# A fused attention, SoLU layer and softplus layer on one core: the planned order computed anew with other transfer costs, LayerNorm weights loaded as rows, and wide early fillers

## The chip, the cores and the metric

The kernel runs on one core of one Trainium2 chip, as one program. The metric is device time in microseconds (us), the median of three runs. One further execution was profiled; all durations below come from it.

## The reference

Three stages follow each other on 4 batches of 576 tokens, 512 wide:

```
scores = q k^T / 8, masked           # 8 heads of 64: heads 0-3 see the last 32 tokens,
attn   = softmax(scores) v           # heads 4-7 every 4th of the last 128
h   = x w_in                         # layer 1: 512 -> 1024
s   = h * softmax(h)
ln  = (s - mean(s)) / sqrt(var(s) + 1e-6) * g_ln
x   = ln w_out                       # 1024 -> 512
out = softplus(x w2_in) w2_out       # layer 2: 512 -> 2048 -> 512
```

The weights arrive as 64-bit floats, q, k and v as 32-bit floats. The output is 2304 x 512, float32.

## The kernel before, in words

**Arithmetic.** The large products run in fp16 with each operand split into a high and a low half, three products for one (high x high, high x low, low x high). A weight piece of 128 x 512 comes in as 512 KB of 64-bit words (`weights`, a DMA of 128 x 1024 words); DVE turns it into 32-bit floats in three steps (`to_f32`: a short TENSOR_SCALAR at L634, two long SCALAR_TENSOR_TENSOR at L637), ACT sums its squares, and when all pieces of a matrix are summed, PE adds over partitions and DVE makes a power-of-two scale (the chain that begins with the TENSOR_REDUCE at L811). Then the high half (ACT or DVE) and the low half (DVE) are written into the resident tile `W`. Parts of `W` and `E` that are not yet in use serve as buffers for raw pieces and for the float32 pieces, so a transfer `W<-in_moe_w_in_dram` is a raw piece on its way in. Layer 1 has eight pieces for `w_in` and eight for `w_out` (names `w1i`, `w1o`), layer 2 four quarters of four and four (`w2i0` to `w2i3`, `w2o0` to `w2o3`).

**Attention.** 28 pairs of blocks (`pair`). The first ten (`pair32`) run in float32: PE turns q and k (L652, four to a block of heads), ACT or DVE copies them from PSUM, PE makes the scores, DVE takes maxima (L1085), ACT the exponentials. The other 18 (`block`) work on fp16 halves, which the DMA turns (`dma_t`, `DMA_TRANSPOSE`). Their results go into the ring `xr`.

**Layers.** 18 tiles of 128 tokens go through layer 1's first product (`m1`: two halves, `ps_w<-W,xr`), the softmax and LayerNorm on DVE (the row maximum at L1320 is its first step) and ACT, and a DMA transpose. Groups of two tiles go through the second product (`y_stage`) and layer 2 (`mlp2`: eight hidden parts and eight output parts).

**The order.** Nothing is issued as written. The functions record operations with costs in a `Plan`; `Plan.order` goes through them with a clock of its own, hands each engine the ready operation with the earliest due time (`TABLE`, one number for each operation, in tenths of us), and the program is then written in that order, with `keep_in_program_order`, so each engine runs its own list in order. All transfers go through SP's list. Costs: `dma_cost(issue, land)`, `moving(packets, size, lag)` for a transfer's share of the DMA engines, `pe_cost` and others for compute. When PE has nothing to do in that plan before 400 us, the plan puts in a filler, emitted at L1572 as eight matmuls of 60 columns that nothing reads:

```
        if o is None:
            for _ in range(8):
                pin(nc.tensor.matmul(banks[1][:, 452:512], eye, eye[:, 0:60], start=False, stop=False, skip_group_check=True))
            continue
```

There are 190 of these groups. `g_ln` (1024 numbers) is loaded with one transfer whose elements are single numbers, into `gT` of 128 x 8; it is the scale in the squares of `w1o` and enters `sg`, the scale of its halves.

Of the kernel before, what the change touches and what calls it, by code (L numbers as in the profile page):

```python
# [65 lines left out]
class Plan:  # L66
# [12 lines left out]
    SWITCH = 1.4  # L79
    CLING = 20.0  # L80
# [64 lines left out]
    def order(self):  # L145
# [13 lines left out]
        idle_at = dict.fromkeys(self.ENGINES, 0.0)  # L159
        over, out, events = set(), [], [0.0]  # L160
        ends = []
        moved = 0.0
        tab = 1
# [7 lines left out]
        while events:  # L171
# [17 lines left out]
            while again:  # L189
                again = False  # L190
                for e in self.ENGINES:
# [56 lines left out]
                    if o.mv:  # L248
                        moved = max(moved, now + c) + o.mv
                        o.t1 = max(o.t1, moved + o.lag)  # L250
# [34 lines left out]
def moving(packets, size, lag=2.4):  # L285

    return packets * (12 + size / 21.0) / 16000, lag
# [3 lines left out]
def kernel(  # L291
# [1316 lines left out]
```

## Time and profile before

| | |
|---|---|
| median of 3 runs | 731.29 us (729.33 to 731.72) |
| the profiled execution | 730.25 us, span of its instructions 728.5 us |
| PE busy | 702.1 us, 96% of the span, fillers included |
| DVE busy | 510.5 us, 70% |
| ACT busy | 457.1 us, 63% |
| DMA | 90.0 MB moved, mean 124 GB/s |

The page cuts the span into 40 equal slices of 18.2 us and gives the busy share of each engine in tenths. DVE's digits are 3 and 5 in the first two slices, 8 and 9 with few exceptions up to the fourteenth, and then fall to between 1 and 9; PE's are 6 in the first slice and 8 or 9 in nearly all others. The DMA engines are at 8 in the first two slices. Busy time of PE counts a matmul from its start to its modelled end, so consecutive matmuls overlap. A row of a timeline gives start, length, engine, line of the kernel, operation and tiles, the count of merged instructions, and in brackets the idle time of the engine before it with what ended that. "PEclk" is the granted clock of PE as a share of 2.4 GHz.

### The profile page before, as it was taken

How to read it: one execution, taken by the hardware profiler on the slowest of the kernel's cores; microseconds unless marked ns; L12 is line 12 of the kernel's file. 1: busy time of each engine (PE TensorE's matmuls, PEld its weight loads, DVE VectorE, ACT ScalarE, POOL GpSimd, SP SyncE). 2: the span in 40 equal slices, each digit the busy share in tenths (PEclk: the TensorE clock that was granted, in tenths of full speed). 3: DMA queues.
4: the chain of work that ended last, by engine and by line, in shares of the span. 5: the costliest groups of instructions: out<-in, count | busy, mean ns of one | idle time of the engine just before them, and what ended most of it. 6: DMA issues, size and time to landing. Idle time of an engine off the chain costs nothing.

```text
span 728.5 us, 17028 instructions
## 1 busy us (share of the span) xinstructions
PE 702.1 (96%) x6697; PEld 508.8 (70%) x6697; DVE 510.5 (70%) x1558; ACT 457.1 (63%) x913; POOL 3.5 (0%) x22
## 2 busy tenths in 40 slices
PE   6988999999999899999999999999999999999997
PEld 6875577877676468777765776776668767657764
DVE  3598999999999883957988973289994372651221
ACT  1677798689899666758886673378972444521112
POOL 1000000000000000000000000000000000000000
PEclk9967999999999999999999999999999999999999
DMA  8869776587995535666776481068641111110001
GB/s 228 239 186 252 229 171 158 151 174 159 186 197 118 149 114 160 163 171 130 169 143 140 102 172 51 10 135 170 133 95 40 34 31 33 31 37 23 1 1 58
DMA packets 187808, 89.98 MB, mean 124 GB/s; under 512 B 158032, under 2 KB 175440, under 8 KB 187728
## 3 DMA queue, kind: packets, MB, share of 16 engines
q1 hardware_dynamic: 187728, 88.90, 52.5%
q8 instruction: 52, 0.85, 0.5%
q14 instruction: 28, 0.23, 0.1%
HBM read 54.53 MB, written 4.72 MB: 81 GB/s over the span
## 4 chain that ended last, share of the span: by engine, by line
PE 68%; DVE 17%; ACT 5%; DMA 5%; issue 3%; POOL 0%; SPq 0%; ACTq 0%; POOLq 0%; DVEq 0%
PE bank L646 35%; PE ps_w L646 28%; DVE W L637 5%; PE bank L1572 4%; DVE E L637 2%; DMA E<-in_moe_w_in_dram 1%; PE bank L652 1%; DMA W<-in_moe_w_out_dram 1%; ACT s L628 1%; DMA pT<-p 1%; DVE s L1194 1%; DVE g L637 1%; ACT L1576 1%; DVE p L640 1%; DVE hl L640 1%
## 5 line engine op out<-in xcount | busy, mean ns | idle before, releaser
L646 PEld LDWEIGHTS <-W 128*128 128x128 f16 x2592 | 252.0, 98 | 35.6
L646 PE MATMUL bank<-y,W 128*128 128x256 f16 x1728 | 197.6, 273 | 0.0
L646 PE MATMUL ps_w<-W,g 128*128 128x512 f16 x864 | 195.4, 379 | 0.0
L646 PEld LDWEIGHTS <-g 128*128 128x128 f16 x864 | 83.2, 98 | 90.3
L646 PE MATMUL ps_w<-W,xr 128*128 128x512 f16 x432 | 100.2, 386 | 2.5 <-DMA xr<-x 2.5
L628 ACT ACTIVATE r<-bank,invC 128x512 f32<-128x512 f32 x72 | 49.2, 685 | 83.5 <-PE bank L646 81.0
L646 PE MATMUL bank<-lnT,W 128*128 128x256 f16 x864 | 96.6, 273 | 0.0
L637 DVE SCALAR_TENSOR_TENSOR g<-r,KR,g 128x512 f16<-128x512 f32 x72 | 53.6, 747 | 40.9 <-ACT g L628 39.1
L1576 ACT ACT_TABLE_LOAD x61 | 78.3, 1283 | 1.1
L646 PEld LDWEIGHTS <-xr 128*128 128x128 f16 x432 | 42.3, 100 | 51.0 <-issue 3.7
L1572 PE MATMUL bank<-eye 128*128 128x60 bf16 x1520 | 55.4, 196 | 8.4 <-issue 2.1
L1572 PEld LDWEIGHTS <-eye 128*128 128x128 bf16 x1520 | 52.5, 102 | 10.3 <-issue 9.9
L628 ACT ACTIVATE s<-s 96x128 f32<-96x128 f32 (+3 forms) x144 | 43.6, 375 | 15.2 <-DVE s L634 11.3
L628 ACT ACTIVATE E<-E 128x768 f32<-128x768 f32 (+3 forms) x52 | 38.3, 737 | 18.1 <-issue 5.5
L632 DVE TENSOR_SCALAR g<-r,KR 128x512 f16<-128x512 f32 x36 | 17.3, 481 | 45.9 <-PE ps_w L646 40.6
L1194 DVE CUSTOM_DVE_ANT_0 s<-bank,band,bsc 96x128 f32<-96x128 f32 (+3 forms) x144 | 39.0, 325 | 7.9 <-PE bank L646 7.7
L628 ACT ACTIVATE y<-bank 128x512 f16<-128x512 f32 x17 | 10.1, 593 | 41.5 <-PE bank L646 41.5
L628 ACT ACTIVATE e<-ps_w,st,bsc 128x1024 f32<-128x1024 f32 x16 | 19.2, 1203 | 24.4 <-DVE st L632 13.5
L637 DVE SCALAR_TENSOR_TENSOR y<-bank,y 128x512 f16<-128x512 f32 x18 | 12.3, 684 | 29.9 <-ACT y L628 29.9
L628 ACT ACTIVATE g<-r,KR 128x512 f16<-128x512 f32 x36 | 25.7, 719 | 9.1 <-PE ps_w L646 8.3
L1320 DVE TENSOR_REDUCE st<-ps_w 128x1 f32<-128x1024 f32 x18 | 21.9, 1219 | 10.0 <-PE ps_w L646 10.0
L637 DVE SCALAR_TENSOR_TENSOR E<-E 128x512 int32<-128x512 int32 x42 | 27.8, 686 | 0.0
(191 smaller groups left out, 864.7 us busy)
## 6 DMA issues: line engine op xcount, KB each, us to landing
E<-in_moe_w_in_dram SPq DMA_DIRECT2D x18, 512.0 KB, 4.7
E<-in_moe_w_out_dram SPq DMA_DIRECT2D x18, 512.0 KB, 4.4
out_dram<-osb SPq DMA_DIRECT2D x18, 256.0 KB, 2.4
E<-in_v_dram SPq DMA_DIRECT2D x9, 384.0 KB, 3.3
E<-in_q_dram SPq DMA_DIRECT2D x9, 384.0 KB, 3.2
E<-in_k_dram SPq DMA_DIRECT2D x9, 384.0 KB, 4.0
W<-in_moe_w_in_dram SPq DMA_DIRECT2D x6, 512.0 KB, 7.5
W<-in_moe_w_out_dram SPq DMA_DIRECT2D x6, 512.0 KB, 4.7
```

The costliest lines, as they stand in the source:

```text
L628: pin(nc.scalar.activation(out=out, in_=in_, func=func, **kw))
L632: pin(nc.vector.tensor_scalar(out=out, in0=in0, scalar1=s1, scalar2=None, op0=op0))
L637: pin(nc.vector.scalar_tensor_tensor(out=out, in0=in0, scalar=s, in1=in1, op0=op0, op1=op1, **kw))
L640: pin(nc.vector.tensor_tensor(out=out, in0=a, in1=b, op=op))
L646: pin(nc.tensor.matmul(out, l, r, start=start, stop=stop))
L652: pin(nc.tensor.transpose(out, in_, eye32[:in_.shape[0], :in_.shape[0]]))
L1194: pin(nc.vector.tensor_tensor_reduce(out=sv()[:rows, h, :nk], in0=sb.t[:rows, h, :nk], in1=band[:rows, 48 - m:48 - m + nk], scale=sc[:rows ...
L1320: ({"DVE": (1.142, 0.14)}, lambda e: pin(nc.vector.tensor_reduce(out=col(0), in_=ph(), axis=AXX, op=ALU.max, negate=True)), [mb], [ps]),
L1572: pin(nc.tensor.matmul(banks[1][:, 452:512], eye, eye[:, 0:60], start=False, stop=False, skip_group_check=True))
L1576: pin(nc.scalar.preload_act_table_set(TABLES[tab]))
```

## The change

Four things change in the code. First, the planner's picture of transfers: engines start at times of their own (`START`), at most eight transfers may be under way (`LANES`, a pool that every SP operation takes a slot of), moving data takes 7% longer per packet, ordinary transfers have a `lag` of 2.2 in place of 2.4 and begin to occupy the DMA engines half a microsecond after their issue begins (`LEAD`), and the transposes get issue times, landing times and lags of their own. Second, with these costs the due times of all operations (`TABLE`, 2522 numbers) are new, so all five lists have a new order. Third, `g_ln` comes as eight rows of 128 numbers into a buffer of the `e` pool, is turned by PE and copied into `gT` by ACT or DVE. Fourth, fillers that stand ahead of the first use of a `ps_w` buffer are one matmul of 512 columns into that buffer.

```diff
@@ class Plan
+    LATE, LEAD = 2.0, 0.5
+    LANES = 8
+    START = {"PE": 4.3, "ACT": 2.0, "DVE": 1.0, "SP": 0.8}
@@ Plan.order
-        idle_at = dict.fromkeys(self.ENGINES, 0.0)
-        over, out, events = set(), [], [0.0]
+        idle_at = dict(self.START)
+        over, out, events = set(), [], sorted(self.START.values())
...
-                        moved = max(moved, now + c) + o.mv
+                        moved = max(moved, now + (c if o.lag > self.LATE else self.LEAD)) + o.mv
@@ moving
-def moving(packets, size, lag=2.4):
-    return packets * (12 + size / 21.0) / 16000, lag
+def moving(packets, size, lag=2.2):
+    return 1.07 * packets * (12 + size / 21.0) / 16000, lag
@@ the table of due times: all of its numbers
-        487, 164, 133, 150, 174, 167, 195, 207, 226, 218, 189, 136, 212, 239, 216, 308, 261, 332, 331, 305, 382,
...
@@ g_ln
-    g_load = P.op("gT", dma_cost(0.5, 4.0), lambda e: dma(gT, g_ln.rearrange("(c p) -> p c", p=128)), due=("w1o", -20))
+    gb, gp = Buf(e_pool), Buf(ps_x)
+    g_load = P.op(
+        "gl", dma_cost(0.4, 2.0), lambda e: dma(gb.t[:K1, 0:128], g_ln.rearrange("(c p) -> c p", p=128)), uses=[gb], mv=moving(8, 512),
+    )
+    g_turn = P.op("gt", pe_cost(0.1), lambda e: turned(gp.t[:, 0:K1], gb.t[:K1, 0:128]), after=[g_load], uses=[gb, gp])
+    g_load = P.op("gT", {**act_cost(K1, psum=1), **dve_cost(K1, x=1)}, lambda e: cast(e, gT, gp.t[:, 0:K1]), after=[g_turn], uses=[gp], due=("w1o", -20))
@@ costs of transfers, one of each kind
-                f"{name}.{i}l", dma_cost(0.4, 3.0),
+                f"{name}.{i}l", dma_cost(0.4, 3.5),
...
-                    f"ld{n}.{x}", dma_cost(0.5, 3.0), load, uses=[buf], mv=moving(4 * cnt, 512),
+                    f"ld{n}.{x}", dma_cost(0.4, 2.4), load, uses=[buf], mv=moving(4 * cnt, 512),
...
-            after=[q_h, q_l, q_d, q_c], uses=[qk, qt], mv=moving(16 * rows, 256, 0.7),
+            after=[q_h, q_l, q_d, q_c], uses=[qk, qt], mv=moving(16 * rows, 256, 1.6),
...
-            after=[ll], uses=[hl, ln], mv=moving(16 * 128, 256, 0.0),
+            after=[ll], uses=[hl, ln], mv=moving(16 * 128, 256, 1.2),
@@ end of the kernel function
+    lanes = Pool("lanes", [None] * P.LANES, fifo=False)
+    for o in P.ops:
+        if "SP" in o.opts:
+            buf = Buf(lanes)
+            o.uses.append(buf)
+            buf.left += 1
+            buf.users.append(o)
     order = P.order()
-    tab = 1
+    tab, unused = 1, True
     mm(banks[1][:, 452:512], eye, eye[:, 0:60], True, True)
     for o in order:
         if o is None:
+            if unused:
+                mm(ps_w.slots[0][0][:, 0], eye, eye.unsqueeze(1).broadcast_to([128, 4, 128]), True, True)
+                continue
             for _ in range(8):
                 pin(nc.tensor.matmul(banks[1][:, 452:512], eye, eye[:, 0:60], start=False, stop=False, skip_group_check=True))
             continue
+        unused = unused and not any(b.pool is ps_w for b in o.uses)
```

What the new order moves is read from the lists of the two programs. Line numbers of the change are higher by 3 at the helpers and by 8 at the reduces.

**SP, the first twelve transfers.** `rq`, `rk`, `qk`, `xd` and parts of `W` are buffers for q, k and v; 128x1024 is a raw weight piece, 128x768 a part of the sweep that measures the sizes of q, k and v. Before:

```order
L655 DMA E<-in_moe_w_in_dram 128x1024
L655 DMA W<-in_v_dram 128x768
L655 DMA rq_107<-in_q_dram 80x4x128
L655 DMA E<-in_moe_w_in_dram 128x1024
L655 DMA W<-in_moe_w_in_dram 128x1024
L655 DMA rk_108<-in_k_dram 80x4x128
L655 DMA W<-in_moe_w_in_dram 128x1024
L655 DMA W<-in_v_dram 128x768
L655 DMA W<-in_k_dram 80x4x128
L655 DMA W<-in_q_dram 80x4x128
L655 DMA xd<-in_v_dram 80x4x128
L655 DMA qk<-in_v_dram 80x4x128
```

Now:

```order
L658 DMA rk_108<-in_k_dram 80x4x128
L658 DMA rq_107<-in_q_dram 80x4x128
L658 DMA W<-in_v_dram 128x768
L658 DMA E<-in_moe_w_in_dram 128x1024
L658 DMA xd<-in_v_dram 80x4x128
L658 DMA qk<-in_v_dram 80x4x128
L658 DMA W<-in_v_dram 128x768
L658 DMA E<-in_moe_w_in_dram 128x1024
L658 DMA W<-in_moe_w_in_dram 128x1024
L658 DMA W<-in_k_dram 80x4x128
L658 DMA W<-in_moe_w_in_dram 128x1024
L658 DMA W<-in_v_dram 128x768
```

The loads of k and q for the first pair moved from the sixth and third place to the first two; the first weight piece moved from the first place to the fourth, and `g_ln` out of this piece of the list.

**PE, from its first instruction to the first turned k and to the first scores.** Rows on `eye` alone are fillers (the very first matmul opens the bank). Before, with 20 groups of eight fillers ahead of the turning of q and 16 more ahead of that of k:

```order
L646 MATMUL bank_137<-eye 128x60
L1572 LDWEIGHTS eye
L1572 MATMUL bank_137<-eye 128x60
...
L652 MATMUL bank_136<-eye_64,rq_107 128x80 x4
L1572 LDWEIGHTS eye
...
L652 MATMUL bank_136<-eye_64,rk_108 128x80 x4
```

Now:

```order
L655 MATMUL bank_136<-eye_64,rk_108 128x80 x4
L649 LDWEIGHTS eye
L649 MATMUL ps_w_140<-eye 128x512
L655 MATMUL bank_138<-eye_64,rq_107 128x80 x4
...
L649 MATMUL bank_136<-band,eye 80x4x80
...
L649 MATMUL bank_138<-band,eye 80x4x80
L649 MATMUL bank_136<-kT,qT 80x80
L649 MATMUL bank_138<-kT,qT 80x80
```

One filler stands between the turnings of k and q, two more (one is shown) ahead of the scores, which begin with the rows on `band`. In all 161 fillers are left of 190: 40 wide ones and 121 groups of eight. 40 stand ahead of the first product of layer 1, where 93 groups stood; 15 groups stand behind the scale of the last quarter `w2i3`, where 4 stood.

**DVE, up to the row maximum of layer 1's first tile** (`st<-ps_w`). The rows on `W` and `E` with 128x512 are steps of conversions of weight pieces. Before:

```order
L634 TENSOR_SCALAR W<-E 128x512
L637 SCALAR_TENSOR_TENSOR W<-E,W 128x512 x2
L634 TENSOR_SCALAR E<-W 128x512
L637 SCALAR_TENSOR_TENSOR E<-W,E 128x512 x2
L634 TENSOR_SCALAR rs_169<-bank_137,bsc_70 96x4
L634 TENSOR_SCALAR W<-E 128x512
L643 RECIPROCAL rs_169<-rs_169 96x4
L637 SCALAR_TENSOR_TENSOR W<-E,W 128x512 x2
L634 TENSOR_SCALAR E<-W 128x512
L637 SCALAR_TENSOR_TENSOR E<-W,E 128x512
L1320 TENSOR_REDUCE st_119<-ps_w_140 128x1
```

Now:

```order
L637 TENSOR_SCALAR W<-E 128x512
L640 SCALAR_TENSOR_TENSOR W<-E,W 128x512 x2
L637 TENSOR_SCALAR W<-W 128x512
L640 SCALAR_TENSOR_TENSOR W<-W 128x512 x2
L637 TENSOR_SCALAR W<-W 128x512
L1093 TENSOR_REDUCE s_113<-bank_136 80x4
L640 SCALAR_TENSOR_TENSOR W<-W 128x512
L1093 TENSOR_REDUCE s_112<-bank_138 80x4
L640 SCALAR_TENSOR_TENSOR W<-W 128x512
L637 TENSOR_SCALAR W<-E 128x512
L1328 TENSOR_REDUCE st_119<-ps_w_140 128x1
```

Ahead of this maximum stood 124 instructions and now stand 110: conversions of layer 2's pieces `w2i0.1`, `w2i0.2`, `w2o0.1`, `w2o0.2` and two steps of `w2i0.0` come behind it now, and one piece of layer 1's `w_out` more stands ahead of it. Ahead of the scale of `w2i3` DVE has 572 instructions where it had 581.

## Rows read from the trace of the kernel before

**Rows 1.** Busy times by stage; columns as in the first line, windows in us.

```profile
core 0: us, PE busy (x) PEld busy (x) DVE busy (x) ACT busy (x) POOL busy (x), PEclk, DMA share, GB/s
0.00:43.70 43.70, 34.14 (x787) 31.85 (x788) 22.78 (x57) 18.43 (x58) 3.53 (x22) 0.95 0.88 233
43.70:77.60 33.90, 29.33 (x256) 22.50 (x255) 30.21 (x69) 26.05 (x77) 0.00 (x0) 0.72 0.81 224
77.60:240.10 162.50, 157.47 (x1895) 119.52 (x1896) 156.45 (x496) 142.90 (x336) 0.00 (x0) 1.00 0.77 170
240.10:273.70 33.60, 31.09 (x222) 18.44 (x220) 28.48 (x79) 20.91 (x34) 0.00 (x0) 0.95 0.43 119
273.70:728.50 454.80, 450.12 (x3542) 316.52 (x3539) 272.60 (x861) 248.84 (x412) 0.00 (x0) 1.00 0.40 89
43.70:60.00 16.30, 15.21 (x167) 13.82 (x167) 16.26 (x39) 13.72 (x38) 0.00 (x0) 0.62 0.61 175
60.00:77.60 17.60, 14.11 (x96) 8.69 (x91) 13.94 (x31) 12.32 (x39) 0.00 (x0) 0.81 1.00 270
```

**Rows 2.** Timeline of DVE, the three marks: start, length, line, operation, idle before.

```profile
43.74 0.17 DVE L811 TENSOR_REDUCE tmp<-bank 128x1 f32<-128x8 f32 x1 [1.11 <-PE bank L1572]
...
77.58 1.22 DVE L1320 TENSOR_REDUCE st<-ps_w 128x1 f32<-128x1024 f32 x1
...
240.11 0.15 DVE L811 TENSOR_REDUCE tmp<-bank 128x1 f32<-128x4 f32 x1
```

**Rows 3.** The same stages, instructions of line L1572 (fillers) alone.

```profile
43.70:77.60 33.90, 4.78 (x96) 4.44 (x95) 0.72 0.81 224
77.60:240.10 162.50, 24.87 (x744) 23.36 (x744) 1.00 0.77 170
240.10:273.70 33.60, 1.04 (x32) 0.97 (x32) 0.95 0.43 119
sum 728.50, PE 55.42 PEld 52.53; mean PE 11.08 PEld 10.51
```

**Rows 4.** Timeline of PE, first 20 us.

```profile
4.02 6.51 PE L1572 MATMUL bank<-eye 128*128 128x60 bf16 x160
10.36 0.47 PE L652 MATMUL bank<-eye,rq 80*128 80x80 f32 x4
...
14.51 3.17 PE L1572 MATMUL bank<-eye 128*128 128x60 bf16 x70 [2.07 <-issue]
17.49 0.77 PE L652 MATMUL bank<-eye,rk 80*128 80x80 f32 x4
```

**Rows 5.** Timeline of DVE, first 43 us.

```profile
5.42 0.43 DVE L634 TENSOR_SCALAR W<-E 128x512 int32<-128x512 int32 x1 [4.36 <-DMA E<-in_moe_w_in_dram]
...
10.87 0.49 DVE L632 TENSOR_SCALAR qT<-bank 128x320 f32<-128x320 f32 x1 [3.57 <-PE bank L652]
...
20.24 0.49 DVE L1085 TENSOR_REDUCE s<-bank 80x4 f32<-80x320 f32 x1 [4.24 <-PE bank L646]
...
39.70 0.41 DVE L634 TENSOR_SCALAR W<-W 128x512 int32<-128x512 int32 x1
```

**Rows 6.** Timeline of SP: the last piece of the first weights is issued.

```profile
24.88 1.88 SPq L655 DMA_DIRECT2D W<-in_moe_w_in_dram  x1
```

**Rows 7.** DMA issues of the first 60 us: size of one, median us to landing.

```profile
W<-in_moe_w_in_dram SPq DMA_DIRECT2D x5, 512.0 KB, 7.6
...
rq<-in_q_dram SPq DMA_DIRECT2D x2, 160.0 KB, 4.4
...
W<-in_k_dram SPq DMA_DIRECT2D x2, 128.0 KB, 7.3
...
gT<-in_moe_g_ln_dram SPq DMA_DIRECT2D x1, 4.0 KB, 7.3
```

**Rows 8.** Groups of DVE by form, 40 to 240 us: a long conversion step.

```profile
L637 DVE SCALAR_TENSOR_TENSOR E<-E 128x512 int32<-128x512 int32 x34 | 22.4, 686 | 0.0
```

**Rows 9.** Waits of PE, 240.1 to 273.7 us: total, times, longest.

```profile
PE ps_w L646 <- DMA xr<-x: 2.5, 1, 2.5
```

**Rows 10.** Waits of SP's queue, 0 to 77.6 us.

```profile
SPq L655 <- ACT E L628: 11.5, 6, 4.4
```

More of the change, by code (lines that the diff above doesn't have):

```diff
@@ L988, in load @@
                         dma(to, s)
-                    two.append(P.op(f"ld{n}.{x}{o}", dma_cost(0.5, 3.0), load, uses=[buf], mv=moving(4 * cnt, 256)))
+                    two.append(P.op(f"ld{n}.{x}{o}", dma_cost(0.4, 2.4), load, uses=[buf], mv=moving(4 * cnt, 256)))
                 lds.append(two)
@@ L1019, in pair @@
         q_t = P.op(
-            f"qT{n}", dma_cost(2.0, 2.4), lambda e: dma_t(qt.t[:, :, :rows], qk.t[:rows, 0:8 * HH].rearrange("p s d -> p (s d)")),
-            after=[q_h, q_l, q_d, q_c], uses=[qk, qt], mv=moving(16 * rows, 256, 0.7),
+            f"qT{n}", dma_cost(2.0, 2.6), lambda e: dma_t(qt.t[:, :, :rows], qk.t[:rows, 0:8 * HH].rearrange("p s d -> p (s d)")),
+            after=[q_h, q_l, q_d, q_c], uses=[qk, qt], mv=moving(16 * rows, 256, 1.6),
         )
@@ L1024, in pair @@
             f"kT{n}", dma_cost(1.6, 2.1), lambda e: dma_t(kt.t[:, :, :kr], qk.t[:kr, 8 * HH:12 * HH].rearrange("p s d -> p (s d)")),
-            after=[k_h, k_l], uses=[qk, kt], mv=moving(8 * kr, 256, 0.7),
+            after=[k_h, k_l], uses=[qk, kt], mv=moving(8 * kr, 256, 1.6),
         )
@@ L1210, in block @@
         p_l = P.op(f"pl{name}", dve_cost(HH * nk), lambda e: tt(pb.t[:rows, 1, :, :nk], sv()[:rows, :, :nk], pb.t[:rows, 0, :, :nk], ALU.subtract), after=[p_h], uses=[s2, pb])
-        pt = P.op(f"pT{name}", dma_cost(1.3, 1.9), lambda e: dma_t(ptb.t[:, :, :rows], pb.t[:rows].rearrange("p a h c -> p (a h c)")), after=[p_l], uses=[pb, ptb], mv=moving(8 * rows, 256, 0.7))
+        pt = P.op(f"pT{name}", dma_cost(1.35, 1.8), lambda e: dma_t(ptb.t[:, :, :rows], pb.t[:rows].rearrange("p a h c -> p (a h c)")), after=[p_l], uses=[pb, ptb], mv=moving(8 * rows, 256, 1.8))
         def values(e):
@@ L1243, in block @@
             x_done[b, 0, 2 * i + o] = [P.op(
-                f"xT{name}", dma_cost(1.3, 1.7), lambda e: dma_t(xr[:, 0, :, r0:r0 + rows], fl()),
-                after=[x_l, *token_wait(t0, t0 + rows)], uses=[x2b], due=due, mv=moving(4 * rows, 256, 0.9),
+                f"xT{name}", dma_cost(1.25, 1.5), lambda e: dma_t(xr[:, 0, :, r0:r0 + rows], fl()),
+                after=[x_l, *token_wait(t0, t0 + rows)], uses=[x2b], due=due, mv=moving(4 * rows, 256, 2.0),
             )]
@@ L1254, in block @@
             unit_ops[u].append(P.op(
-                f"xT{name}", dma_cost(1.3, 1.7), lambda e: dma_t(xd.t[:, :, r, :], fl()), after=[x_l], uses=[x2b, xd], mv=moving(4 * rows, 256, 0.9),
+                f"xT{name}", dma_cost(1.25, 1.5), lambda e: dma_t(xd.t[:, :, r, :], fl()), after=[x_l], uses=[x2b, xd], mv=moving(4 * rows, 256, 2.0),
             ))
```

287 rows, old and new, of the table TABLE are left out of this document.

## The prediction

> **What bounds the kernel now.** The page's slices come first: DVE stands near its limit up to about 255 us, behind that PE alone does, so PE's 96% over the span is a mean over two different stages. Then the busy times by stage [rows 1]. I cut the span at marks that can be found in both programs [rows 2]: the reduce that makes the scale of the first weights (DVE L811, 43.74 us), the first row maximum of layer 1 (L1320, 77.58 us), the scale of the last quarter of layer 2's input weights (L811, 240.11 us); and at 273.7 us, where layer 1's third group begins its second product. Between 43.7 and 240.1 us DVE is busy 30.2 of 33.9 and 156.5 of 162.5 us. From 273.7 us on PE is busy 450.1 of 454.8 us, and most of the rest is the output's tail. So DVE sets the pace until 240 us and PE behind it. PE's stage has a fixed length, since the arithmetic does not change: **what the change is worth is how much earlier DVE comes through its first 240 us**, corrected for waits that PE meets later.
>
> PE's fillers (L1572) took 55.4 us [rows 3]. A filler costs nothing where PE would have waited; it costs where it stands ahead of work that is ready. That is so at the start [rows 4]: 160 fillers ran for 6.51 us, until the first turning of q began at 10.36 us; more of them, the last 70 behind a hole of 2.07 us, ran until the first turning of k at 17.49 us. DVE works in order and stood meanwhile behind instructions that needed these results, 3.57 and 4.24 us [rows 5]. Had it gone through, it would not have begun the last piece of the first weights at 39.70 us only. That piece was issued at 24.88 us, with 1.88 us of issue time [rows 6], and such a transfer landed in 7.6 us by the median [rows 7]: it lay ready from about 34 us.
>
> **The change part by part.** *Start to the first scale.* The order puts k and q of the first pair at SP's head and three fillers ahead of the first scores in place of 39 groups of eight; the forty earliest are single and 512 wide. A 160 KB load of q landed in 4.4 us [rows 7], so the scores can begin near 7 us; their first maximum was at 20.24 us [rows 5]. DVE's own work up to the scale hardly changes: four copies of q and k go to ACT (three like the 0.49 us of [rows 5], one of a larger block, 0.7 us), four small instructions of 0.2 to 0.5 us come in; 22.8 us [rows 1] become some 22.2. It had 20.9 us idle. What limits it now are the loads: eight weight pieces of 524 KB and all that stands ahead of the last of them make 6.8 MB; at this stage's 233 GB/s [rows 1] that is 29 us, with 2 us until the first bytes about 31 us. Behind the last landing come its conversion, pair 2's maxima and the sum, 4 us as before (39.70 to 43.74 us), and 1 us for slips. First scale at 36.0 us, gain 7.7. Bounds: no gain, if the loads run at the 175 GB/s of the next 16 us, and 11 us at the 270 GB/s of the 18 us behind those [rows 1].
>
> *To the first maximum of layer 1.* Conversions of layer 2's pieces that stood ahead of it now stand behind it: nine long steps at 0.686 us [rows 8] and four short ones at 0.41 us [rows 5], 7.8 us, and small ones of 1.9 us; one piece of layer 1's output weights (1.8 us) and a copy (0.6 us) come in. 30.2 less 7.3 is 22.9 us; I leave the stage's idle 3.7 us as it was. The mark falls at 62.6 us, 15 earlier, but 7.3 us of that is work put off. The loads bear this: 14.1 MB must have come by then, 62 us at the 229 GB/s that the first 77.6 us had on average [rows 1].
>
> *To the scale at 240 us.* DVE has 572 instructions ahead of this mark where it had 581. By the means of their groups in this trace they are 3.7 us shorter in sums of durations; those overlap (247.7 us of them in 209.4 us of busy time), so 3.1 us. Left behind the first maximum: 209.4 - 3.1 - 22.2 - 22.9 = 161.2 us. With the stage's idle 6.1 us the mark comes at 62.6 + 167.3 = 229.9 us, **10.2 us earlier**. If that idle time doubled, the gain would be 4, if it went to nothing 16.
>
> *To PE's full stretch.* Here the stage took 33.6 us with 31.1 us of PE busy: 1.0 us of filler [rows 3] and 2.5 us of waiting for a turned x [rows 9] were lost. In the new order 15 groups of eight stand here, at 33 ns a filler (24.87 us for 744 [rows 3]) 4.0 us, just where the order expects such a wait. I take 0.5 us more loss; bounds 0 (they cover it) and 3 (the wait comes on top).
>
> *PE's full stretch.* There are no fillers, before or now. In the new order the scores of an attention block stand at least 17 us of PE work ahead of its values (8 us before), the values at least 8 us ahead of layer 1 (6 before), layer 1 at least 20 us ahead of the second product (19 before). Nothing is closer than what ran without a wait in [rows 1], so I take 0; bounds 0 and 3 us, the size of the one long wait [rows 9].
>
> *g as rows.* One DMA issue takes the place of one; a turning on PE and a copy on DVE come in, 0.2 us, counted above. g's transfer landed in 7.3 us [rows 7] and its first reader ran at 46 us: covered before, and no price now. The bounds are nothing and those 7 us of a queue, if they held up other loads; I take nothing, since loads of 128 KB beside it landed in the same time.
>
> *PE's clock with fewer fillers.* 161 groups remain of 190, and 40 rather than 93 stand ahead of layer 1's first product. The granted clock was 0.62 of full between 43.7 and 60 us and 0.81 up to 77.6 us [rows 1], so PE falls to 1.2 GHz here already, between transposes and waits, and DVE was 89% busy all the same. The Trainium skill's page "TensorE: Matmul & The Clock Gate", Part 1, says that the low clock is the default and that only activity lifts it; by it fewer fillers mean more time at 1.2 GHz, and the trace agrees in kind. I take no loss, since DVE sets this stage; the loss is a rival below.
>
> Sum: 10.2 - 0.5 = 9.7 us off the profiled execution's span of 728.5 us, 718.8; 1.75 us lie around the span (730.25 in all): **720.5 us.** The median of the runs, 731.29, is 1.04 above this execution; I leave that aside.
>
> **The rivals.** *Loads fall behind (slower).* SP issues in order, and in the first 77.6 us it waited over and over for a reader to let go of a buffer, 11.5 us for one ACT line alone [rows 10]. The new order wants 14.1 MB by the first maximum. If held buffers block more of the queue, the rate falls; at 182 GB/s the mark stays at 77.6 us, and with 167 us behind it the scale comes at 245 us: 4.8 + 0.5 us later, 735.5. Below 182 GB/s it is slower, and the stretch at 175 GB/s [rows 1] shows that such rates occur. Against it: the order now counts eight transfers in flight and longer landings.
>
> *The clock (no difference).* PE's work besides fillers between 43.7 and 77.6 us was 24.6 us [rows 1, 3] at a mean clock of 0.72. All of it at 1.2 GHz would be 35 us, more than the 26.6 us that I give DVE: PE takes over, the mark comes at 71 us, and 8.5 of the 10 us are gone: 729. For it speaks the 0.62 of [rows 1], against it that no stage shows half clock throughout. By the rule of the Trainium skill named above this is what waits on PE do.
>
> *Gain given back (little).* DVE's work before 240 us falls by only 3.1 us. If the idle time saved at the start comes back in the middle, in waits like those of [rows 5], 3 us remain: 727.5.
>
> *Nearly all idle time goes.* DVE waits 4.36 us for its first load [rows 5]; if of its 30.7 idle us up to 240 us only 11 remain, the scale comes 23 us earlier: 707.5.
>
> **How the numbers follow.** Forecast (gain of 6 to 14 us) 0.50, nearly all idle time gone 0.18, gain given back 0.12, clock 0.08, loads behind 0.12. A measurement of this kernel can tell about 0.3% (2.2 us) from no change. The first two and most of the third are faster: 0.79; the clock and the rest of the third are the same: 0.09; slower 0.12. Range: from 706 (all idle time gone, and a little more) to 733 (half of the price of late loads); what lies outside is the worse part of the slow rival and some of the fast end.
>
> **What would show it.** Right: first scores near 7 us on PE, the L811 reduce of the first scale near 36 us, layer 1's first maximum near 63 us, the scale of the last quarter near 230 us, PE without long waits behind 265 us. Wrong at the loads: SP waiting for ACT or PE, and under 200 GB/s in the first 60 us. Wrong at the clock: half clock through the first 70 us, and DVE waiting for PE's banks. Wrong at the last step: PE waits of over 3 us behind 280 us. Wrong as a whole: if DVE's idle time up to the scale of the last quarter is no smaller than 30.7 us.

## The result, and the profile after

The changed kernel takes 723.77 us (median of 5 runs, 722.45 to 724.25); the kernel before took 730.54 us in 5 runs beside it (727.85 to 731.72). The ratio is **0.991, interval 0.9886 to 0.9934**: faster by 0.9%, and 3.3 us longer than the 720.5 us predicted. Ratios, here and below, are taken over the fast runs of both kernels, so they differ a little from the quotient of the medians shown. The profiled execution took 724.25 us with a span of 722.4 us.

Busy times of the changed kernel by stage, cut at the same marks as [rows 1] and with its columns:

```profile
0.00:34.80 34.80, 25.21 (x171) 15.48 (x172) 21.69 (x57) 18.15 (x54) 3.52 (x22) 0.88 0.97 273
34.80:59.00 24.20, 21.04 (x138) 14.30 (x137) 23.94 (x56) 19.82 (x60) 0.00 (x0) 0.82 0.87 225
59.00:231.30 172.30, 164.38 (x2016) 126.28 (x2015) 161.74 (x501) 147.85 (x352) 0.00 (x0) 0.99 0.71 174
231.30:266.40 35.10, 33.75 (x326) 21.57 (x325) 32.51 (x87) 22.65 (x44) 0.00 (x0) 1.00 0.51 135
266.40:722.40 456.00, 450.58 (x3542) 316.67 (x3539) 270.25 (x853) 251.64 (x433) 0.00 (x0) 1.00 0.41 88
```

The three marks on DVE's timeline, as [rows 2] has them (the program is longer, so lines 811 and 1320 of before are 819 and 1328 here):

```profile
34.82 0.20 DVE L819 TENSOR_REDUCE tmp<-bank 128x1 f32<-128x8 f32 x1
...
58.98 1.22 DVE L1328 TENSOR_REDUCE st<-ps_w 128x1 f32<-128x1024 f32 x1
...
231.32 0.16 DVE L819 TENSOR_REDUCE tmp<-bank 128x1 f32<-128x4 f32 x1 [0.25 <-PE bank L649]
```

The start on PE, against [rows 4]: k is turned at 4.20 us (17.49 before) and the first scores run at 7.27 us, between a few wide fillers.

```profile
4.20 0.80 PE L655 MATMUL bank<-eye,rk 80*128 80x80 f32 x4
4.79 0.63 PE L649 MATMUL ps_w<-eye 128*128 128x512 bf16 x1
5.21 0.74 PE L655 MATMUL bank<-eye,rq 80*128 80x80 f32 x4
...
7.27 1.36 PE L649 MATMUL bank<-kT,qT 64*80 64x80 f32 x16
```

Set beside the prediction's own stages, the lengths are (us):

| stage, up to | before | predicted | after | after - predicted |
|---|---|---|---|---|
| first scale | 43.7 | 36.0 | 34.8 | -1.2 |
| first maximum of layer 1 | 33.9 | 26.6 | 24.2 | -2.4 |
| scale of the last quarter | 162.5 | 167.3 | 172.3 | +5.0 |
| PE's full stretch | 33.6 | 34.1 | 35.1 | +1.0 |
| end | 454.8 | 454.8 | 456.0 | +1.2 |
| span | 728.5 | 718.8 | 722.4 | +3.6 |

So the first two stages gave more than forecast, and the third took back more than that. Of its 172.3 us DVE was busy 161.74 (161.2 forecast): it stood still for 10.6 us, not 6.1. DVE's waits in that stage (total, times, longest):

```profile
DVE xr L643 <- PE bank L1590: 4.1, 5, 1.3
DVE tmp L819 <- PE bank L1590: 1.6, 3, 0.6
DVE xr L643 <- ACT xf L631: 0.9, 1, 0.9
```

The first two name line 1590: the late **fillers**, whose results nobody reads, 5.7 us together. Before, such waits on fillers made up 2.4 us of the same stage. The view of that line says who waited for fillers over the whole span, ACT too:

```profile
DVE xr L643: 4.1, 5
ACT xr L631: 1.9, 3
DVE tmp L819: 1.6, 3
ACT xf L631: 1.5, 2
```

The program's order shows why. A filler goes to columns 452 to 512 of `banks[1]`, in this program `bank_137`; attention puts the turned x and other results into other columns of the same bank, as into three more. DVE's low halves of x, with what each waits for (numbers of its list ahead):

```
141 L643 TENSOR_TENSOR xr<-bank_138,xr 128x2x72 [waits Activation_49]
151 L643 TENSOR_TENSOR xr<-bank_137,xr 128x2x72 [waits PE_49,Activation_49]
217 L643 TENSOR_TENSOR xr<-bank_137,xr 128x2x96 [waits PE_49,Activation_49]
222 L643 TENSOR_TENSOR xr<-bank_139,xr 128x2x96 [waits Activation_49]
```

In the fillers' bank they wait for PE once more. ACT has read the bank for the high half; then a group of eight fillers may write it, and DVE's read of the same bank comes after them. The dependency in this program goes by tile, not by columns. The Trainium skill's page "PSUM — Partial Sum Buffer", in "PSUM bank collisions raise a hardware error", asks for that: PSUM is to be guarded by bank and group of 32 partitions (in the simple version by bank), not by address, since PE and another engine collide in disjoint columns too. Fillers and these reads both cover all 128 partitions, so by it the remedy is another bank and not a dependency by columns; the runs below bear out the first half, and none tried the second.

### The profile page after: what moved, and what is told of

Read it like the earlier page. It is cut to its first block, busy times and chain, and to the rows that moved or that the text cites. A ratio compares the mean times of both kernels' runs of the same rounds, so it can differ in the third digit from the quotient of the medians.

```text
span 722.4 us, 15990 instructions
## 1 busy us (share of the span) xinstructions
PE 695.0 (96%) x6186; PEld 494.3 (68%) x6186; DVE 510.1 (71%) x1550; ACT 460.1 (64%) x938; POOL 3.5 (0%) x22
## 4 chain that ended last, share of the span: by engine, by line
PE 77%; DVE 13%; DMA 5%; ACT 4%; issue 1%; SPq 0%; DVEq 0%; ACTq 0%
PE bank L649 39%; PE ps_w L649 32%; PE bank L1590 3%; DVE W L640 3%; DMA E<-in_moe_w_in_dram 2%; DMA W<-in_v_dram 1%; PE bank L655 1%; DVE E L640 1%; ACT xr L631 1%; DMA kT<-qk 1%; ACT E L631 1%; DVE xr L643 1%; ACT xf L631 1%; DMA xd<-x 1%; DVE s L1202 1%
## 5 line engine op out<-in xcount | busy, mean ns | idle before, releaser
L649 PEld LDWEIGHTS <-W 128*128 128x128 f16 x2592 | 252.0, 98 | 35.8 <-issue 0.4
L649 PE MATMUL bank<-y,W 128*128 128x256 f16 x1728 | 197.9, 273 | 0.3 <-DVE y L640 0.3
L649 PE MATMUL ps_w<-W,g 128*128 128x512 f16 x864 | 195.0, 379 | 0.0
L649 PEld LDWEIGHTS <-g 128*128 128x128 f16 x864 | 83.5, 98 | 90.9
L649 PE MATMUL ps_w<-W,xr 128*128 128x512 f16 x432 | 97.9, 379 | 0.0
L649 PE MATMUL bank<-lnT,W 128*128 128x256 f16 x864 | 97.4, 273 | 0.0
L631 ACT ACTIVATE r<-bank,invC 128x512 f32<-128x512 f32 x72 | 49.2, 685 | 71.9 <-PE bank L649 63.8
L649 PEld LDWEIGHTS <-xr 128*128 128x128 f16 x432 | 41.6, 99 | 44.9 <-issue 0.2
L631 ACT ACTIVATE s<-s 96x128 f32<-96x128 f32 (+3 forms) x144 | 43.7, 375 | 15.9 <-DVE s L637 15.7
L1590 PE MATMUL bank<-eye 128*128 128x60 bf16 x968 | 34.2, 191 | 7.7 <-DVE xr L643 2.5
L1590 PEld LDWEIGHTS <-eye 128*128 128x128 bf16 x968 | 31.9, 98 | 9.9 <-issue 9.4
L635 DVE TENSOR_SCALAR g<-r,KR 128x512 f16<-128x512 f32 x29 | 13.9, 478 | 35.1 <-PE ps_w L649 30.6
L631 ACT ACTIVATE g<-r,KR 128x512 f16<-128x512 f32 x43 | 30.8, 720 | 5.1 <-PE ps_w L649 4.2
L631 ACT ACTIVATE hl<-e,st 128x1024 f16<-128x1024 f32 x18 | 22.2, 1235 | 15.9 <-DVE st L640 9.7
L631 ACT ACTIVATE xf<-bank,rs 80x64 f32<-80x64 f32 (+1 forms) x104 | 23.6, 305 | 11.4 <-DVE rs L646 8.6
```

Of the source, the lines that this page charges most:

```text
L631: pin(nc.scalar.activation(out=out, in_=in_, func=func, **kw))
L635: pin(nc.vector.tensor_scalar(out=out, in0=in0, scalar1=s1, scalar2=None, op0=op0))
L649: pin(nc.tensor.matmul(out, l, r, start=start, stop=stop))
```

## The experiments

**Theory**: the new order and the wide early fillers each free time, and late fillers in a bank that others read give part of it back. **Rivals**: the early fillers alone are the whole gain; the new order gains nothing whatever the fillers do; the loads bound the start; the clock does. Times are medians beside runs of the kernel before on the same chip; all marks are starts on DVE's timeline.

| run | median (before) | ratio, interval | first scale | first maximum | last quarter's scale | span |
|---|---|---|---|---|---|---|
| after | 723.8 (730.5) | 0.991, 0.989 to 0.993 | 34.8 | 59.0 | 231.3 | 722.4 |
| e3 | 723.2 (731.6) | 0.990, 0.987 to 0.993 | 37.5 | 70.6 | 233.6 | 720.5 |
| e1 | 726.9 (731.6) | 0.994, 0.992 to 0.996 | 40.4 | 64.5 | 236.3 | 726.0 |
| e4 | 723.6 (731.6) | 0.990, 0.988 to 0.993 | 34.4 | 59.5 | 231.0 | 721.2 |
| e5 | 716.2 (731.6) | 0.980, 0.977 to 0.983 | 35.7 | 60.2 | 225.2 | 713.6 |
| e10 | 724.4 (732.6) | 0.990, 0.986 to 0.994 | 38.4 | 63.8 | 234.5 | 724.2 |
| e8 | 723.8 (732.6) | 0.989, 0.985 to 0.993 | 36.9 | 69.9 | 234.4 | 722.0 |
| e6 | 716.6 (732.6) | 0.979, 0.975 to 0.983 | 34.9 | 59.0 | 225.7 | 716.3 |
| e2 | 723.8 (732.6) | 0.988, 0.984 to 0.993 | 36.8 | 61.2 | 231.5 | 724.0 |
| e7 | 719.0 (732.3) | 0.980, 0.978 to 0.983 | 36.4 | 60.8 | 227.2 | 718.0 |
| e9 | 719.4 (732.3) | 0.982, 0.979 to 0.985 | 36.0 | 61.3 | 227.8 | 717.1 |

None of these kernels leaves out arithmetic that the output needs; fillers compute nothing.

**e3, the early fillers alone.** The kernel before, in its own order, with the new rule for fillers ahead of the first use of `ps_w`.

```diff
-    tab = 1
+    tab, unused = 1, True
...
+            if unused:
+                mm(ps_w.slots[0][0][:, 0], eye, eye.unsqueeze(1).broadcast_to([128, 4, 128]), True, True)
+                continue
...
+        unused = unused and not any(b.pool is ps_w for b in o.uses)
```

> The kernel before, with nothing changed but its fillers ahead of layer 1's first product: one of 512 columns into ps_w in place of eight of 60 into the bank that attention uses. My theory of the start: 36 groups stand ahead of the first turnings of q and k; at about 0.22 us each in place of 0.33 us, and without the 2 us hole of fetching, k is turned near 13 us (17.5 before), the first scale falls near 40 us (43.7) and the time drops by 2 to 4 us, to about 727.5. Rival, that only the order of the loads counts: first scale within 1 us of 43.7, time 729.5 to 731.5.

It took 723.2 us, as much off as the whole change and more than twice what was expected; the first scale, too, came earlier than expected (37.5 us, not 40). Its marks (lines 811 and 1320 as in [rows 2]):

```profile
37.53 0.17 DVE L811 TENSOR_REDUCE tmp<-bank 128x1 f32<-128x8 f32 x1 [0.38 <-PE bank L646]
...
70.55 1.22 DVE L1320 TENSOR_REDUCE st<-ps_w 128x1 f32<-128x1024 f32 x1
...
233.61 0.15 DVE L811 TENSOR_REDUCE tmp<-bank 128x1 f32<-128x4 f32 x1
```

The scale comes 6.2 us earlier than before, the first maximum 7.0, the last quarter's scale 6.5: what the start gives is kept, with no order changed.

**e1 and e10, the changed kernel with narrow early fillers.** In e1 the early ones are eight of 60 columns in `banks[1]` again; in e10 eight of 60 in the `ps_w` buffer.

```diff
-            if unused:
-                mm(ps_w.slots[0][0][:, 0], eye, eye.unsqueeze(1).broadcast_to([128, 4, 128]), True, True)
-                continue
```

```diff
-                mm(ps_w.slots[0][0][:, 0], eye, eye.unsqueeze(1).broadcast_to([128, 4, 128]), True, True)
+                for _ in range(8):
+                    mm(ps_w.slots[0][0][:, 0, 0:60], eye, eye[:, 0:60], True, True)
```

> The changed kernel with its forty earliest fillers as groups of eight of 60 columns in bank 1, as they were. If they lie ahead of ready work, 40 times 0.1 us and the waits in bank 1 come back: first scale 1 to 2 us later than 34.8, layer 1's first maximum 2 to 4 us later than 59.0, time 724.5 to 727. Rival, that at the new order PE has time to spare there: 723 to 724.5, marks within 1 us.

> The changed kernel with its forty earliest fillers as groups of eight of 60 columns, but written into ps_w. It parts the two things that the change did to them. If the bank counts: 723 to 724.5, as the changed kernel. If the width counts: 726 to 727.5, as the run with narrow ones in bank 1.

In the new order the early fillers matter less: e1 is 3.2 us above the changed kernel's median, by ratios 0.3% (the intervals overlap), and its first scale 5.6 us late, which is more than either expectation had. It is also the new order with the old fillers, and 0.6% below the kernel before. What the bank and the width have in it stays open. In the medians e10, with the other bank alone, can't be told from the changed kernel, but by its ratio not from e1 either. In its profile (of a run of 726.1 us) the first scale comes 2.0 us earlier than in e1 and still 3.6 us later than in the changed kernel, and the two later marks, too, lie nearer to e1's.

**e4, no late fillers; e5, late fillers where no buffer lies.** e4 leaves the 121 late groups out. In e5 each late group goes into a place in PSUM that no buffer holds at that point of the order, and is left out where there is none (7 groups).

```diff
-            for _ in range(8):
-                pin(nc.tensor.matmul(banks[1][:, 452:512], eye, eye[:, 0:60], start=False, stop=False, skip_group_check=True))
```

```diff
+    places = {id(p): t for t, p in zip(banks, taken)}
+    places.update({id(s[4]): s[0][:, 0] for s in ps_w.slots})
...
-            for _ in range(8):
-                pin(nc.tensor.matmul(banks[1][:, 452:512], eye, eye[:, 0:60], start=False, stop=False, skip_group_check=True))
+            free = [x for x in places if not held[x]]
+            if free:
+                t = places[min(free, key=used.get)]
+                for _ in range(8):
+                    mm(t[:, 0:60], eye, eye[:, 0:60], True, True)
...
```

> The changed kernel without the 121 groups of fillers behind the first use of ps_w (the 40 wide ones stay). Theory F, the fillers write bank 1, which attention reads, so DVE and ACT wait for fillers and fillers for them: the 4.1 us of DVE xr and 1.6 us of DVE tmp waiting behind fillers go, DVE comes to the scale of the last quarter 3 to 6 us earlier (231.3 now), time 718 to 721. Rival C, the clock: without fillers PE is granted 1.2 GHz for much of 59 to 250 us, layer 1's and 2's products take up to twice as long, time 728 or more. Rival D, the fillers fill time that nobody needs: 723 to 724.5.

> The changed kernel, the later fillers (groups of eight, 60 columns) written into whichever PSUM place no buffer holds at that point of the list, seven groups left out for want of one. Theory F: nearly all DVE and ACT waits for fillers go, the clock stays up as it is, last quarter's scale 3 to 6 us earlier, time 718 to 721. Rival D, DVE's own work sets the middle and the waits named there hide other ones: 723 to 724.5. Rival C says nothing against it, since the fillers stay: equal to now.

e4 alone looks as if late fillers did nothing. Busy times of e4 by stage, then three stretches inside the third:

```profile
34.40:59.50 25.10, 20.73 (x133) 13.30 (x132) 24.16 (x56) 20.32 (x61) 0.00 (x0) 0.82 0.89 227
59.50:231.00 171.50, 153.78 (x1174) 108.06 (x1172) 161.36 (x501) 147.23 (x350) 0.00 (x0) 0.91 0.68 174
84.40:94.60 10.20, 9.43 (x35) 5.53 (x36) 7.88 (x32) 8.87 (x23) 0.00 (x0) 0.50 0.68 175
101.50:111.70 10.20, 8.14 (x39) 4.21 (x38) 8.79 (x20) 10.01 (x30) 0.00 (x0) 0.50 0.88 204
```

Without fillers PE falls to 1.2 GHz there, 0.91 over the stage where the changed kernel has 0.99 (0.50 is 1.2 GHz), and DVE's waits in it are now on PE's real work:

```profile
DVE s L1093 <- PE bank L649: 2.5, 2, 2.2
DVE tmp L757 <- PE bank L649: 2.0, 1, 2.0
DVE xr L667 <- PE bank L655: 2.0, 1, 2.0
```

That is 6.5 us, about the 5.7 us that DVE stood behind fillers in the changed kernel. The three longest end at 95.8, 112.6 and 132.5 us, each in or just behind a stretch at 0.50. e5 has neither kind of wait. Its stages and the longest of DVE's waits in the third:

```profile
0.00:35.70 35.70, 27.96 (x171) 19.23 (x172) 21.75 (x57) 18.29 (x54) 3.53 (x22) 0.77 0.95 261
35.70:60.20 24.50, 21.60 (x133) 14.71 (x132) 24.11 (x56) 20.06 (x61) 0.00 (x0) 0.77 0.91 230
60.20:225.20 165.00, 160.43 (x1965) 123.15 (x1964) 161.19 (x501) 147.47 (x351) 0.00 (x0) 1.00 0.75 182
```

```profile
DVE tmp L819 <- PE bank L649: 0.6, 2, 0.3
DVE E L637 <- DMA E<-in_moe_w_in_dram: 0.5, 1, 0.5
```

The stage is 165.0 us, DVE idle 3.8 of it instead of 10.6, the clock full. (The fillers of e5 run at the line of a helper that real work uses too, L649, so waits for them can't be named apart; all of DVE's idle time is those 3.8 us.) The stage behind it is 33.5 us instead of 35.1. 716.2 us **beats both kernels**: 2.0% under the kernel before and, by the two ratios, 1.1% under the changed one. So the late fillers do earn their place, by the clock, and lost in the changed kernel by their bank what they had earned.

**e8, the same place for late fillers in the old order** (e3 with e5's edit; 17 of 97 groups left out), and **e6**, e5 with one filler of 512 columns in place of eight of 60.

```diff
+                mm(t[:, 0:512], eye, eye.unsqueeze(1).broadcast_to([128, 4, 128]), True, True)
```

> The kernel before in its old order, with single fillers of 512 columns ahead of the first use of ps_w and the later groups written into whichever PSUM place no buffer holds (17 of 97 groups left out for want of one). It asks what the new order is worth when fillers hold up nobody. Theory O, the new order comes through DVE's stage sooner once fillers are out of its way: this kernel gains only the 2 to 4 us of its own waits behind fillers over the run with wide early fillers (723.2), 719 to 721.5, and stays 3 us or more behind the changed kernel with free places (716.2). Rival N, the order is worth nothing beside the fillers: within 1.5 us of 716.2.

> The changed kernel, every later filler a single matmul of 512 columns into a PSUM place that no buffer holds. If what counts is where a filler writes, it equals the run with groups of eight in free places: 716.2, within 1.5 us. If the number of instructions counts too (121 against 968), it is 1.5 to 3 us faster.

The old order gains nothing by it: 723.8 us, not the 719 to 721.5 expected, last quarter's scale at 234.4 us (e3 233.6). It had only 2.4 us of such waits to lose, and it met new ones. Its third stage up to that scale; PE's fillers into banks from 90 to 102 us, with the idle time before them; the clock behind that; a wait of DVE:

```profile
69.90:234.40 164.50, 157.92 (x1758) 118.99 (x1759) 156.59 (x496) 142.58 (x336) 0.00 (x0) 0.97 0.73 168
L646 PE MATMUL bank<-eye 128*128 128x60 bf16 x40 | 2.4, 226 | 2.8 <-DVE xr L640 2.8
91.00:100.00 9.00, 9.00 (x66) 7.51 (x66) 6.42 (x24) 7.16 (x18) 0.00 (x0) 0.50 0.61 149
DVE st L1320 <- PE ps_w L646: 1.6, 1, 1.6
```

DVE is idle for 7.9 us of this stage (6.5 in e3). A place that no buffer holds at that point of the list can still have a reader at work: PE stood 2.8 us before a filler until DVE had read its bank, ran at half clock behind it, and DVE then waited 1.6 us for layer 1's product. So the new order is 7.6 us ahead (716.2 against 723.8; by the ratios 0.980 and 0.989, 0.9%; against e6, on the same chip as e8, 1.0%) with the late fillers out of the shared bank, of which some 2 us may be e8's fillers and not its order. Beside wide early fillers and late ones in the shared bank it is worth nothing (after against e3). e6 equals e5 in time: for the late fillers the place counts, and the width has no price that can be measured.

**e2, g as single numbers again**, in the same place of the order, without the turning and the copy.

```diff
-        "gl", dma_cost(0.4, 2.0), lambda e: dma(gb.t[:K1, 0:128], g_ln.rearrange("(c p) -> c p", p=128)), uses=[gb], mv=moving(8, 512),
+        "gl", dma_cost(0.4, 2.0), lambda e: dma(gT, g_ln.rearrange("(c p) -> p c", p=128)), uses=[gb], mv=moving(8, 512),
...
```

> The changed kernel with g loaded as single numbers straight into its place, at the same point of SP's list; no turning, no copy. My theory: no difference, 723 to 724.5, since its first reader comes 30 us later. Rival, that 1024 single numbers hold up the loads beside them: first scale 1 to 4 us later than 34.8, time 724.5 to 727.

723.8 us: no difference that can be told. Its first scale lies 2.0 us later than the changed kernel's, as the rival had it, and the last quarter's only 0.2; so nothing of that lasted, and a mark in a single profile at the start can be off by some 2 us without a cause that the end shows.

**e7, the awaited piece first; e9, no early fillers**, both on e6. In the changed kernel DVE's longest wait at the start is for one weight piece:

```profile
DVE W L637 <- DMA E<-in_moe_w_in_dram: 7.9, 1, 7.9
```

```diff
+    order.sort(key=lambda o: o is None or o.name != "w1i.3l")
```

```diff
-                mm(ps_w.slots[0][0][:, 0], eye, eye.unsqueeze(1).broadcast_to([128, 4, 128]), True, True)
```

> The kernel of e6 (late fillers 512 wide in a place that no buffer holds) with the last piece of the first layer's weights moved to the head of SP's work; nothing else is moved. In the profile of the changed kernel DVE stood still 7.9 us once, for this piece. Theory: the loads fill their engines up to there (273 GB/s in the first 34.8 us), so that a piece that comes earlier makes others later by as much, and q, k and the first scores wait for these: 716.5 us, within 1 us either way, and the first scale of layer 1 within 1 us of where e6 has it. Rival: the wait is a matter of this one piece's place; then the first scale comes 2 to 3 us earlier and the time is 713.5 to 714.5.

> The kernel of e6 without its forty wide early fillers; the late ones stay. Theory: the early fillers do no work that anything needs, PE has time to spare until the first scale, and what the clock costs there lies in PE's spare time: 716.5 us, within 1.5 us either way. Rival: they buy the clock under the first work; then the granted clock of the first 60 us falls by 0.05 or more from e6's, the first scale comes 2 us or more later, and the time is 718.5 to 722.

e7's waits up to 60 us:

```profile
DVE s L1093 <- PE bank L649: 5.7, 3, 4.3
DVE W L637 <- DMA E<-in_moe_w_in_dram: 4.1, 1, 4.1
```

The wait moved on to the scores (e6 has 1.0 us there and 7.3 for the piece), the first scale came at 36.4 us (34.9 in e6), and the ratio is e6's within its interval. Both expectations missed: the median is 719.0 us (715.5 to 720.1), above the theory's 716.5, and the scale came later, not earlier. One piece's place does not help. That fits loads that bound this stretch (the DMA engines are at 0.97 in it in the changed kernel), but no run made the loads faster or fewer. e9's median is within 0.4 us of e7's beside the same runs of before; by the ratio to before it is 0.3% above e6, inside e6's interval. Its marks lie 1.1, 2.3 and 2.1 us behind e6's, its span 0.8, though e6's profile is of a run of 718.1 us. The median is where the rival wanted it (e7, which has the fillers, is there too); the first scale, 1.1 us later, is where the theory did. So the early fillers are worth little in this order, and no run settles how much. The granted clock in the profile of e9 is 1.00 up to 79 us, and that is misleading. Groups of PE of e9, from 20 to 27 and from 48 to 55 us (count, busy time, mean ns):

```profile
L649 PE MATMUL bank<-kT,qT 64*80 64x80 f32 x16 | 1.4, 348 | 0.0
...
L649 PE MATMUL ps_w<-W,xr 128*128 128x512 f16 x6 | 2.8, 631 | 0.0
```

and the same two forms in the changed kernel:

```profile
L649 PE MATMUL bank<-kT,qT 64*80 64x80 f32 x16 | 0.8, 240 | 0.0
...
L649 PE MATMUL ps_w<-W,xr 128*128 128x512 f16 x13 | 3.1, 379 | 0.0
```

348 against 240 ns and 631 against 379: without early fillers PE ran at the low level from its start until about 55 us. e6 itself is not at full clock throughout: it has 379 ns for the second form, but 348 for the first, and its rows read

```profile
20.00:27.00 7.00, 7.00 (x50) 5.23 (x48) 4.05 (x13) 2.44 (x11) 0.00 (x0) 0.55 1.11 323
34.00:41.00 7.00, 7.00 (x39) 5.99 (x39) 6.82 (x20) 6.85 (x21) 0.00 (x0) 0.50 1.13 281
```

By rows and durations together some 25 of its first 59 us were at the low level (an estimate). So the early fillers spare PE some 30 us of half clock there, and without them DVE came to the first maximum only 2.3 us later.

**Not tried.** The planner's new costs with the old due times, or the reverse, so it is open how the new order's gain divides between them; and fillers in a part of the shared bank with a dependency by columns.

## Why the prediction was right and where it failed

- *Which side, and where.* Right: DVE sets the pace up to the full stretch, PE's stretch is fixed, the gain is what DVE saves up to 240 us. 723.8 us lies in the range.
- *Start to the first scale, 36.0 us.* 34.8. The loads ran at 273 GB/s, not at the 233 of [rows 1] (the upper bound had 270). That they are the limit now fits DVE's one long wait, 7.9 us for a weight piece, and e7, but is not proved. The prediction took fillers and order together; the runs part them: with old fillers the new order has the scale at 40.4 us (e1), with new fillers the old order has it at 37.5 (e3), against 43.7 before. So the fillers are the larger part.
- *To the first maximum, 26.6 us.* 24.2. The busy time was 23.9 us (22.9 forecast), but the 3.7 us of idle time that I left "as it was" became 0.3.
- *To the scale at 240 us: the failed step.* "With the stage's idle 6.1 us" carried a number over from the old order. 10.6 us were measured. The busy term held (161.7 against 161.2 us). The sentence behind the error is "a filler costs nothing where PE would have waited": a filler also holds its bank against readers of other columns, 5.7 us of DVE's waits here; with the fillers elsewhere 3.8 us of idle time remain (e5).
- *To the full stretch, +0.5 us.* +1.5. The forecast took the 15 groups to cover most of the old wait, and they came, at 4.1 us of PE; but PE waited once more, now for the fillers' bank:

```profile
PE bank L1590 <- ACT xf L631: 1.1, 1, 1.1
PE bank L1590 <- DVE rs L635: 0.3, 1, 0.3
```

e5 has no such wait: 33.5 us, 33.45 of them PE busy. Besides, 4.0 us of DVE's work had been put off past the mark (28.5 us in [rows 1], 32.5 now), which I had not counted; whether DVE limits this stage too is not shown.
- *PE's full stretch, nothing.* +1.2 us. It doesn't follow the order: the stretch lasts 454.8 us (before) and 456.5 (e3) in the old order, 456.0 (after) and 454.8 (e5) in the new one. What it follows stays open.
- *g, nothing.* No difference could be told (e2).
- *The clock, no loss.* Borne out for the first 60 us as far as the runs go (e9, with some 30 us more at the low level there, is 0.3% above e6, inside its interval). The rival was wrong in place: the clock matters in the third stage, where e4 lost by it what it won, and where the changed kernel's fillers kept it at 0.99.
- *Rivals.* "Loads fall behind" fell: 273 and 225 GB/s in the two stages up to 59 us, and the wait of [rows 10], 11.5 us up to the first maximum, is 3.4 up to the same mark now (`ACT E`). SP's longest wait there, for PE's reads, stayed about as it was: 7.2 us after 7.7. "Gain given back" was half true: idle time did come back in the middle, but behind fillers, and 6.1 us of the span stayed saved. "Nearly all idle time goes" is where e5 points: 18.1 us of idle up to the last quarter's scale, 23.9 in the changed kernel, 30.7 before.

The total came out near because the first two stages were 3.6 us better than forecast while the three behind them were 7.2 us worse; so far its nearness is luck.

## What to carry to other kernels

An instruction that only keeps a clock up has a price by its destination: put it where no other engine is still to read or reading (e5, and e8 for what happens otherwise), and read in the profile who waited for its line. When removing such work changes nothing, look for two effects that cancel before calling it idle (e4 against e5). A change of several parts wants its smallest part run alone in the old kernel: here a few lines on fillers, alone, brought as much as the whole change with its new order of 2522 operations, and beside them the order showed a gain of its own only after the late fillers were mended.

## What was not expected of the hardware

- The granted clock in the rows of a profile stays at 1.00 until the first recorded change, though PE ran at the low level from its start: 348 ns against 240 for the same matmul in e9, and in the changed kernel's first scores too, 354 ns. The Trainium skill's page "TensorE: Matmul & The Clock Gate", Part 1, has the low level as the default, and these durations agree where the clock's own rows do not.
- Some 30 us more of half clock at the start cost little (e9's marks lie 1.1 to 2.3 us behind e6's), while some 30 us of half clock between 77 and 132 us cost about 6 (e4's last quarter's scale at 231.0 us, e5's at 225.2): it depends on who waits for PE there, and the clock's mean doesn't tell (0.995 in e9's rows, 0.966 in e4's).
